# A new written order of steps for a Nystrom attention and feed-forward kernel, with a changed planner's clock

## The chip, the cores and the metric

The kernel runs on one core of one Trainium2 chip. The metric is the device time of one execution in microseconds (us). The median of several runs is compared before and after the change; lower is better.

The engines are called as in the profile: PE is TensorE (PEld its weight loads), DVE is VectorE, ACT is ScalarE, POOL is GpSimd, SP is SyncE, whose queue issues most of the DMAs.

## The reference

There are 8 batches of 576 rows, with 8 heads of 64 columns. For each head, 32 landmarks are the means of 18 rows each, and three softmax matrices and an iterated inverse give the attention:

```
q_lm, k_lm = means of 18 rows of q, of k
A, Bm, C = sm(q, k_lm), sm(q_lm, k_lm), sm(q_lm, k)
Z = Bm^T / (norm1(Bm) * norminf(Bm))
for _ in range(6): Z = 2 Z - Z Bm Z
x = A Z C v                      # heads side by side: 576 x 512 for each batch
xn = (x - mean) / sqrt(var + 1e-6) * g
out = x + relu(xn @ w1) @ w2     # w1 512 x 2048, w2 2048 x 512
```

Everything comes in and goes out as fp32; the kernel multiplies in fp16.

## The kernel before

**Stages.** The batches are taken in sets: batch 0 in code of its own, then (1), (2), (3, 4), (5, 6) and (7). For a set, q, k and v are loaded (tiles stg, a ring of six buffers that W1, W2 and the mixed W2 share), cast to fp16 by POOL or sometimes ACT (tiles nat and natv), turned by DVE (xT) and summed to landmarks (DVE's part, POOL's asum, or products on PE, bank<-nat,pairs). Then come the score products (psec, psea), their exponentials (ec, ea), the Gram product and six iterations for Z (tile st: a small product on PE, then one DVE operation, six times in a row), the product with v (pscv), and zt and zcbd, from which the rows of the attention's output are made (xblk). DVE measures each block of 128 rows (bn_stats into six, bn_aggr into stats).

**The feed-forward part.** The first layer does not use the rows: it multiplies zt with W1 (two products of heads give m), then m with ea, 16 chunks of hidden units for each batch (psh), which are passed through Relu into hT. The second layer multiplies hT with W2, 16 matmuls for a block of 128 rows, and adds the result, scaled, to xblk, which is then stored. For batches 4 to 7 four of the blocks are replaced by seven products of mixed quarters (bank<-w2mix and so on); DVE makes the mixed hT, POOL the mixed W2.

**The centerings.** For batches 0 and 1 the mean over W1's rows (less) is subtracted when m is copied out. From batch 2 on W1 itself is centered: `center_w1` (line 1484) adds less to two of the four parts of a quarter of W1, 1024 elements in each of 128 partitions, in one DVE operation. There are eight of these (DVE w<-w,less). Batch 2's first layer may not begin before all eight are written (line 1864, `first_layers`).

**What sets the order.** Each engine runs its instructions in the order in which the program lists them, and semaphores hold an instruction until its inputs are there. The order is written by hand: `ORDER` (line 1828) is a list of symbols with counts, run by `run` (line 1922). A symbol is a step:

- 0 to 4 are streams: 0 the attentions (from set (1) on), 1 the totals on PE, 2 the first layers, 3 the rows of batch 0, 4 the second layers. A step passes one `yield` of its stream. A step of 4 is mostly one matmul of 512 columns, or one of 256 in the seven products; a step of 2 mostly four matmuls of 288.
- J is a turn or a sum on DVE, M measures a block, C is a centering, X mixes a part of hT, W a part of W2, K casts and L loads one tile of 576 KB.

So "42 2 L" means two steps of the second layer, one of the first and a load. A step that can't be written yet (its input isn't made, or its buffers are all pinned) goes to a list `late` and is tried again after each following step. A buffer stays pinned from its load until its cast is written. `settle` writes the stores of finished blocks as soon as the clock says that they are done; they go to SP's queue, as the loads do.

**The planner's clock.** While the program is written, `Clock` (line 85) notes every instruction and keeps an estimate of when each engine is free and each tile is written. This is a calculation in Python; no instruction comes from it. But choices hang on it: whether ACT or DVE copies a result (`sooner`, line 635, and `chunk`, line 1540), whether an attention step is an iteration or something beside it, when a store goes out, whether a filler matmul is put in (`warm`), and whether ACT takes a cast. It knows that some DVE operations of 1024 elements and POOL's operations hold each other up (`locks`, and `took` for n of 1024).

Ahead of `run` stands a fixed part: batch 0's attention, the loads of W1 and W2 and their casts. It is not in the list.

Of the kernel before, what the change touches and what calls it, by code (L numbers as in the profile page):

```python
# [20 lines left out]
def kernel(  # L21
# [20 lines left out]
    MCH = HID // P  # L42
# [30 lines left out]
    def keys_of(ap):  # L73
        n = name_of(ap)
        if n not in parted:
            return [n]
        at = [ap.offset % list(ap.ap)[0][0]]
        for step, k in list(ap.ap)[1:]:
            if step >= parted[n]:
                at = [o + step * i for o in at for i in range(k)]  # L80
        if n in mixed_:
            return [f"{n}:{o // parted[n]}:{int(o % parted[n] >= 256)}" for o in at]
        return [f"{n}:{o // parted[n]}" for o in at]

    class Clock:
# [5 lines left out]
        def __init__(self):  # L91
            self.free = dict.fromkeys(("PE", "DVE", "Activation", "Pool", "SP"), 0.0)
            self.wrote, self.used, self.begun = {}, {}, {}
            self.small, self.lanes, self.wire = False, {}, 0.0
            self.cells, self.count, self.mark, self.fetched, self.ahead = [], 0, 95, 0.0, 0.0
            self.loads, self.pool = [], []
            self.locks = []
            self.free['PE'], self.issued = 1500.0, 0

        def share(self, span=3400.0):  # L100
# [31 lines left out]
        def took(self, i, e, n, m):  # L132
            op = type(i).__name__
            if e == "Activation":
                return 300 if n < 8 else 190 + (1.07 if name_of(i.outs[0].bass_ap).startswith("ec_") else 0.79) * n
            if e == "Pool":
                if n == 1024 and name_of(i.outs[0].bass_ap) in mixed_:
                    return 2080
                if "Ptr" in op:
                    return 100 + 1.29 * n  # L140
                return 100 + 0.92 * n if "Copy" in op else 280 + 1.76 * n
            if "Copy" in op and n in (256, 384, 512, 640) and name_of(i.outs[0].bass_ap).startswith("xT"):
                return 90 + 0.58 * n
            if n == 1152 and "Copy" in op:
                return 760
            if n == 576 and "Copy" in op and name_of(i.outs[0].bass_ap).startswith("nat_"):
                return 400
            if "Stats" in op:
                return 690 if m > 100 else 180
            if n >= 512 and (n == 576 or op == 'InstTensorCopy'):  # L150
                return 100 + 1.13 * n
            if n == 1024:
                last = max([b for a, b in self.pool if a <= self.ready < b] + [0.0])
                next_ = self.locks and self.ready - self.locks[-1][1] < 150
                queued = (690 if self.free["Pool"] <= self.ready else
                          1600 if next_ and self.free["Pool"] > self.ready + 1000 else 1000)
                return max(queued, last - self.ready + 560)
            if n == 256 and "Ptr" in op and name_of(i.outs[0].bass_ap).startswith("xblk"):
                return 480
            if "Transpose" in op:  # L160
                return 110 + 1.15 * n
            return 140 + 1.15 * max(n, m if "Reduce" in op else 0)

        def note(self, i):
            e = str(i.engine).rsplit(".", 1)[-1]
# [3 lines left out]
            count = []  # L169
            for dims in size:  # L170
                n = 1
# [63 lines left out]
                    done = self.lanes[lane[0]] + 160  # L235
            else:
                start = max(self.free[e], ready)
                if e == "Pool":
                    for a, z in self.locks:
                        if a <= start < z:  # L240
                            start = z
                self.ready = start
                done = start + self.took(i, e, count[0], max(count[1:] + [0]))
                self.free[e] = done - self.OVERLAP[e]
                if e == "Pool":
                    self.pool = self.pool[-8:] + [(start, done)]
                    self.free["DVE"] += sum(done - a for a, _ in self.locks[-2:] if start < a < done)
# [1444 lines left out]
    def mix_ahead():  # L1692
# [6 lines left out]
        if i == 0:  # L1699
            n = hTs[b].name  # L1700
            mixed_.update((name_of(s1), name_of(s2), n))
            for seen in (clock.wrote, clock.used):
                seen.update({f"{n}:{m}:{h}": seen[f"{n}:{m}"] for m in range(MCH) for h in range(2)
                             if f"{n}:{m}" in seen})
            mix(s1, h21, h22, ALU.add, k)
        elif i == 1:
# [111 lines left out]
    def scaled_by_pe():  # L1818
# [7 lines left out]
    begun_first = [0]  # L1826

    ORDER = (
# [18 lines left out]
    ).split()  # L1847
    JOB, MEASURE, CENTER, MIX, MIX_W2, CAST, LOAD = range(5, 12)

# [173 lines left out]
```

## Time and profile before

| | us |
|---|---|
| three runs: median (lowest to highest) | 262.17 (261.54 to 262.8) |
| profiled execution | 262.2 |
| its span, first to last instruction | 260.5 |
| busy: PE, DVE, ACT, POOL | 251.2, 206.9, 172.3, 139.7 |

The mean granted TensorE clock is 1.00. In a line of the timeline the columns are start and length in us, engine, line, operation and tiles, with a count; the square bracket holds the idle time of the engine just before and what ended it. A line of the chain has start, length, and engine with the tile written. All helpers record at lines 316 (DVE, ACT, POOL) and 322 (PE), so the tiles' names tell instructions apart. "w<-w,less" is a centering, "m<-less,zsum,bank" a copy with the mean subtracted, "bank<-w,hT" the second layer, "psh<-ea,m" the first.

### The profile page before, as it was taken

The page shows a single profiled execution, that of the slowest core. Times are in us where ns is not written, and L with a number is a line of the kernel's source. Part 1 is how long each engine was busy: PE and PEld are TensorE (multiplying, and loading weights), DVE is VectorE, ACT ScalarE, POOL GpSimd, SP SyncE. Part 2 cuts the span into 40 slices and gives each one's busy share as a digit, 9 for nine tenths or more (in the row PEclk, how much of TensorE's full clock was granted, in tenths as well). Part 3 has the DMA queues.
Part 4 walks back from the last instruction along what each step waited for, and adds up shares of the span by engine and source line. Part 5 has one row for each costly group of instructions (what it writes and reads, how often), then busy time and mean ns, then how long its engine had stood idle before and what let it go on. Part 6 is the DMA issues. An engine that isn't in the chain of part 4 may idle for free.

```text
span 260.5 us, 8627 instructions
## 1 busy us (share of the span) xinstructions
PE 251.2 (96%) x3551; PEld 167.8 (64%) x3551; DVE 206.9 (79%) x470; ACT 172.3 (66%) x330; POOL 139.7 (54%) x165
## 2 busy tenths in 40 slices
PE   6899999999999999999999999999999999999994
PEld 6645754556455574546655466688878876788883
DVE  2667966999989978999997794987495997398862
ACT  2798975559767987289987668636788835786000
POOL 5188779999990989679999996300000006000000
PEclk9999999999999999999999999999999999999999
DMA  6999999997966899658961101200240025100605
GB/s 243 374 397 371 402 402 383 359 331 228 347 195 204 279 374 284 184 168 242 286 154 43 37 10 40 63 22 0 57 108 3 4 55 119 33 3 3 160 21 184
DMA packets 23119, 46.70 MB, mean 179 GB/s; under 512 B 2980, under 2 KB 3240, under 8 KB 23080
## 3 DMA queue, kind: packets, MB, share of 16 engines
q1 hardware_dynamic: 22600, 45.50, 54.3%
q10 hardware_dynamic: 480, 0.66, 0.8%
q8 instruction: 28, 0.46, 0.7%
q14 instruction: 11, 0.09, 0.1%
HBM read 36.70 MB, written 9.44 MB: 177 GB/s over the span
## 4 chain that ended last, share of the span: by engine, by line
PE 70%; DVE 13%; DMA 8%; POOL 4%; issue 1%; ACT 1%; SPq 1%; POOLq 0%
PE bank L322 45%; PE psh L322 18%; DMA stg<-in_q_dram 5%; DMA wstg<-in_moe_w_ch_dram 3%; POOL w L316 3%; PE pscv L322 2%; DVE m L316 2%; DVE xblk L316 2%; DVE w L316 2%; PE psd L322 2%; DVE part L316 1%; DVE six L316 1%; POOL ea L316 1%; DMA out_dram<-xblk 1%; DVE st L316 1%
## 5 line engine op out<-in xcount | busy, mean ns | idle before, releaser
L322 PE MATMUL bank<-w,hT 128*128 128x512 f16 (+3 forms) x528 | 110.1, 335 | 0.2 <-POOL w L316 0.2
L316 ACT ACTIVATE hT<-psh 128x576 f16<-128x576 f32 x124 | 78.1, 652 | 19.1 <-PE psh L322 16.9
L322 PE MATMUL psh<-ea,m 128*128 128x288 f16 x512 | 80.0, 286 | 0.3 <-DVE m L316 0.2
L322 PEld LDWEIGHTS <-hT 128*128 128x128 f16 x656 | 60.2, 98 | 29.9 <-issue 5.0
L322 PEld LDWEIGHTS <-m 128*128 128x128 f16 x512 | 49.4, 98 | 18.8 <-issue 1.3
L316 POOL TENSOR_TENSOR ea<-ea,lns 128x576 f16<-128x576 f16 x16 | 20.9, 1314 | 56.5 <-ACT lns L316 56.4
L316 DVE SCALAR_TENSOR_TENSOR xblk<-bank,rstd,xblk 128x256 f32<-128x256 f32 (+2 forms) x77 | 38.9, 539 | 12.2 <-PE bank L322 11.9
L316 POOL CAST nat<-stg 128x1152 f16<-128x1152 f32 x26 | 30.3, 1182 | 9.3 <-DVE xT L316 7.0
L316 DVE BATCH_NORM_STATS2 six<-xblk 128x6 f32<-128x512 f32 x36 | 24.3, 674 | 0.1
L316 POOL CAST natv<-stg 128x1152 f16<-128x1152 f32 (+1 forms) x17 | 19.3, 1162 | 8.5 <-DMA stg<-in_v_dram 8.4
L316 DVE STREAM_TRANSPOSE xT<-nat 128x576 uint32<-128x576 uint32 x28 | 21.3, 760 | 0.0
L316 DVE SCALAR_TENSOR_TENSOR st<-st,bank 128x128 f16<-128x128 f16 (+3 forms) x36 | 13.2, 366 | 7.1 <-PE bank L322 6.9
L316 ACT ACTIVATE lns<-psd 128x576 f32<-128x576 f32 x16 | 10.3, 645 | 12.3 <-PE psd L322 12.1
L322 PE MATMUL bank<-w2mix,hT 128*128 128x256 f16 x128 | 18.0, 273 | 0.0
L322 PE MATMUL bank<-w2mix 128*128 128x256 f16 x128 | 17.3, 273 | 0.0
L316 DVE TENSOR_REDUCE part<-xT 128x32 f16<-128x576 f16 x20 | 14.4, 741 | 0.0
L322 PEld LDWEIGHTS <-w2mix 128*128 128x128 f16 x128 | 12.3, 98 | 1.9
L316 ACT ACTIVATE ea<-psea 128x576 f16<-128x576 f32 x14 | 8.3, 648 | 7.9 <-PE psea L322 7.9
L322 PEld LDWEIGHTS <-st 32*32 32x32 f16 (+1 forms) x380 | 6.8, 90 | 9.9 <-DVE st L316 5.1
L316 ACT ACTIVATE ec<-psec 128x256 f16<-128x256 f32 (+1 forms) x42 | 12.0, 427 | 1.7 <-PE psec L322 1.6
L316 ACT COPY xblk<-bank 128x512 f32<-128x512 f32 (+1 forms) x16 | 9.3, 592 | 5.6 <-PE bank L322 5.6
L316 POOL TENSOR_TENSOR asum<-nat 128x512 f32<-128x512 f16 x10 | 12.5, 1249 | 0.8
(132 smaller groups left out, 372.4 us busy)
## 6 DMA issues: line engine op xcount, KB each, us to landing
stg<-in_q_dram SPq DMA_DIRECT2D x16, 576.0 KB, 6.4
stg<-in_k_dram SPq DMA_DIRECT2D x15, 576.0 KB, 5.6
out_dram<-xblk SPq DMA_DIRECT2D x66, 128.0 KB, 2.4
wstg<-in_moe_w_ch_dram SPq DMA_DIRECT2D x16, 512.0 KB, 7.5
stg<-in_v_dram SPq DMA_DIRECT2D x5, 576.0 KB, 7.4
stg<-in_v_dram SPq DMA_DIRECT2D x40, 72.0 KB, 3.1
stg<-in_v_dram SPq DMA_DIRECT2D x6, 288.0 KB, 6.2
stg<-in_v_dram SPq DMA_DIRECT2D x12, 144.0 KB, 3.1
```

The lines of the kernel that those rows point to most:

```text
L316: return lambda *args, **kw: keep(getattr(self.engine, op)(*args, **kw))
L322: keep(nc.tensor.matmul(o, l, r, start=start, stop=stop, tile_position=(rb, cb), skip_group_check=(skip or cb != 0)))
```

## The change

The list is replaced by another of the same steps: 1337 in both, with the same number of each symbol. Beyond order, these things differ: the old list begins with the first layer of batch 0 and spreads its loads, while the new one begins with ten loads; the eight centerings, the measurements, casts and attention steps have other places among the steps of the first and second layers.

The places of the eight centerings, by the number of second-layer steps (symbol 4) written before each: 18, 21, 50, 58, 63, 90, 93, 94 in the old list and 16, 27, 49, 57, 87, 91, 92, 93 in the new. The step that holds batch 2's Gram product (the 22nd of stream 0) comes after 66 in the old and 70 in the new.

In the clock, DVE's operations on 1024 elements now look back at all of POOL's operations that run at the time; POOL's operations already noted are pushed back when a DVE operation holds them (`hold_pool`); a POOL operation that starts within such a DVE operation ends later instead of starting later; all DVE tensor_tensor operations of 1024 elements count, not only the centerings; and ACT's scaling of W1 is taken at 750 ns. A mixed hT is tracked in three parts of 256 columns (the third shorter) instead of two.

The diff, cut to its core:

```diff
@@ keys_of
-            return [f"{n}:{o // parted[n]}:{int(o % parted[n] >= 256)}" for o in at]
+            return [f"{n}:{o // parted[n]}:{int(o % parted[n] // 256)}" for o in at]
@@ Clock.took
+                if n == 512 and name_of(i.outs[0].bass_ap).startswith("w1_16"):
+                    return 750
...
-                last = max([b for a, b in self.pool if a <= self.ready < b] + [0.0])
-                next_ = self.locks and self.ready - self.locks[-1][1] < 150
-                queued = (690 if self.free["Pool"] <= self.ready else
-                          1600 if next_ and self.free["Pool"] > self.ready + 1000 else 1000)
-                return max(queued, last - self.ready + 560)
+                return max([690] + [p[1] - self.ready + 545 for p in self.pool
+                                    if p[0] <= self.ready < p[1]])
...
+        def hold_pool(self, start, done):
+            free = 0.0
+            for p in self.pool:
+                if p[0] <= start:
+                    continue
+                was = p[1]
+                if p[0] < free:
+                    p[0] = free
+                    p[1] = p[0] + p[2]
+                if p[0] < done:
+                    p[1] = max(p[1], done + p[2] - 140)
+                free = p[1] - self.OVERLAP["Pool"]
...
+            self.free["Pool"] = max(self.free["Pool"], free)
@@ Clock.note
-                    for a, z in self.locks:
-                        if a <= start < z:
-                            start = z
+                    done = max([done] + [z + took - 140 for a, z, _ in self.locks if a <= start < z])
+                    for lock in self.locks:
+                        if start < lock[0] < done and done + 545 > lock[1]:
+                            lock[1] = done + 545
+                            self.free["DVE"] = max(self.free["DVE"], lock[1] + self.worked - lock[2] - 80)
...
-                if e == 'DVE' and count[0] == 1024 and writes[0] in parted_w1:
-                    self.locks = self.locks[-4:] + [(start, done)]
+                if e == 'DVE' and count[0] == 1024 and "TensorTensor" in type(i).__name__:
+                    self.locks = self.locks[-6:] + [[start, done, self.worked]]
+                    self.hold_pool(start, done)
@@ ORDER (the first lines of each)
-        "2 3 4 211 M 32 25 3 J 0 J3 22 J3 2 1 2 3 22 L 2 M 2 1 2 1 2 J 2 1 4 2 3 L 4 0 42 2 0 "
-        "4 23 0 4 L 0 4 02 4 L M 4 04 L 4 0 K 0 L 42 2 M 0 43 L 42 K 0 C 22 J 0 4 K J K 42 C "
-        "4 2 J 42 2 L 42 0 2 J 43 2 4 M 43 K 45 J 4 L J2 K J 0 2 J 4 J L2 0 4 2 L 4 L 2 M 4 2 "
-        "M L 4 2 4 K M 2 L 4 2 4 2 4 2 0 M 2 42 2 K C 48 0 2 C 45 C 4 L 4 K 4 0 4 K 4 K2 0 47 "
-        "1 04 L 43 02 4 J 43 0 43 L2 K 4 0 4 J 4 1 0 42 K 2 C L 42 0 L 4 C 4 C 44 K 0 L 2 4 J "
...
+        "L5 3 L5 0 210 3 M 3 25 M 4 22 J 2 J 23 J 2 J 2 M J 2 J 2 1 32 M J 0 2 1 2 1 4 2 1 2 "
+        "4 3 J 42 0 2 4 22 0 4 03 42 0 2 03 4 02 2 4 0 K 44 K 4 C 42 0 22 42 0 K J2 4 K 4 2 4 "
+        "2 44 C 0 J 4 0 4 K 2 J 2 J2 44 M2 42 J 0 43 J K J 4 J 2 M2 K 4 M 4 2 42 22 42 2 42 "
+        "22 42 2 C 2 0 4 L 43 L 44 L C 4 2 4 L 2 K L 0 42 K 43 L2 44 K3 4 L 4 02 44 02 L 4 0 "
+        "43 0 4 0 J 1 0 4 0 2 43 K2 4 0 2 4 J K 42 1 0 C 4 L 43 0 C M 4 K C 4 C L 43 K 4 0 L "
...
```

Both lists end with 181 steps of the second layer in a row.

More of the change, by code (lines that the diff above doesn't have):

```diff
@@ L96, in __init__ @@
             self.loads, self.pool = [], []
-            self.locks = []
+            self.locks, self.worked = [], 0.0
             self.free['PE'], self.issued = 1500.0, 0
@@ L162, in took @@
             return 140 + 1.15 * max(n, m if "Reduce" in op else 0)
+        def hold_pool(self, start, done):
[10 more added lines that the diff above has]
+                free = p[1] - self.OVERLAP["Pool"]
+                if p[1] > was:
+                    for at, names in ((self.used, p[3]), (self.wrote, p[4])):
+                        for n in names:
+                            if at.get(n) == (was, "Pool"):
+                                at[n] = p[1], "Pool"
+            self.free["Pool"] = max(self.free["Pool"], free)
         def note(self, i):
@@ L237, in note @@
                 start = max(self.free[e], ready)
+                self.ready = start
+                took = self.took(i, e, count[0], max(count[1:] + [0]))
+                done = start + took
                 if e == "Pool":
-                    for a, z in self.locks:
-                        if a <= start < z:
-                            start = z
-                self.ready = start
-                done = start + self.took(i, e, count[0], max(count[1:] + [0]))
-                self.free[e] = done - self.OVERLAP[e]
-                if e == "Pool":
-                    self.pool = self.pool[-8:] + [(start, done)]
-                    self.free["DVE"] += sum(done - a for a, _ in self.locks[-2:] if start < a < done)
-                if e == 'DVE' and count[0] == 1024 and writes[0] in parted_w1:
-                    self.locks = self.locks[-4:] + [(start, done)]
+                    done = max([done] + [z + took - 140 for a, z, _ in self.locks if a <= start < z])
[3 more added lines that the diff above has]
+                            self.free["DVE"] = max(self.free["DVE"], lock[1] + self.worked - lock[2] - 80)
+                    self.pool = self.pool[-24:] + [[start, done, took, reads, writes]]
+                self.free[e] = done - self.OVERLAP[e]
+                if e == "DVE":
+                    self.worked += done - start - self.OVERLAP[e]
+                if e == 'DVE' and count[0] == 1024 and "TensorTensor" in type(i).__name__:
+                    self.locks = self.locks[-6:] + [[start, done, self.worked]]
+                    self.hold_pool(start, done)
             for n in reads:
@@ L1702, in mix_ahead @@
             for seen in (clock.wrote, clock.used):
-                seen.update({f"{n}:{m}:{h}": seen[f"{n}:{m}"] for m in range(MCH) for h in range(2)
+                seen.update({f"{n}:{m}:{h}": seen[f"{n}:{m}"] for m in range(MCH) for h in range(3)
                              if f"{n}:{m}" in seen})
```

26 rows, old and new, of the table ORDER are left out of this document.

## The prediction

> **What bounds the kernel now.** I read the engine table of the page and its chain first.
>
> ```profile
> span 260.5 us, 8627 instructions
> ...
> PE 251.2 (96%) x3551; PEld 167.8 (64%) x3551; DVE 206.9 (79%) x470; ACT 172.3 (66%) x330; POOL 139.7 (54%) x165
> ...
> PE 70%; DVE 13%; DMA 8%; POOL 4%; issue 1%; ACT 1%; SPq 1%; POOLq 0%
> ```
>
> TensorE (PE) is busy for all but 9.3 us of the span and holds 70% of the chain that ended last. A busy PE need not be a streaming one, so the next view is the timeline of a stretch in the middle.
>
> ```profile
> 179.72 0.65 PE L322 MATMUL psh<-ea,m 128*128 128x288 f16 x4
> 180.21 0.38 PE L322 MATMUL bank<-w2mix,hT 128*128 128x256 f16 x2
> 180.43 0.65 PE L322 MATMUL psh<-ea,m 128*128 128x288 f16 x4
> ```
>
> Four matmuls of 288 columns are followed after 0.49 us, and two of 256 columns after 0.22 us. That is 0.122 and 0.110 us a piece, in proportion to the columns (0.42 and 0.43 ns each), so nothing but columns is being paid for. The record of a group runs 0.16 us past the start of the next (0.65 against 0.49). So whatever the page calls PE idle hides up to 0.16 us more at each place. Next, the busy time by stage (columns: stretch; its length; then each engine's busy time and count).
>
> ```profile
> 18.20:50.00 31.80, 30.85 (x420) 17.50 (x421) 24.84 (x64) 23.83 (x49) 27.62 (x29) 1.00 1.03 390
> 50.00:66.00 16.00, 16.00 (x156) 9.73 (x160) 15.76 (x31) 12.06 (x23) 15.29 (x18) 1.00 0.91 275
> 66.00:74.00 8.00, 7.01 (x129) 3.60 (x108) 7.70 (x20) 4.75 (x13) 7.45 (x9) 1.00 0.92 331
> 74.00:250.00 176.00, 175.85 (x2475) 120.59 (x2474) 145.63 (x318) 120.79 (x234) 79.83 (x80) 1.00 0.40 113
> ```
>
> The third number is PE. What precedes 18.2 us is written ahead of the list of steps, and behind 250 us runs the end of the second layer, 181 steps in a row in both lists. Between lies what an order can touch: PE idles 0.95 us in 18.2 to 50, nothing in 50 to 66, 0.99 us in 66 to 74, and 0.15 us in the 176 us after. That is 2.1 us, and with 0.16 us hidden at some seven places about 3.2 us. VectorE (DVE) is full from 50 to 74, but PE waits for it only in the one stretch of 8 us.
>
> **The change part by part.** The list keeps its 1337 steps, and as many of each kind (830 of the second layer, 165 of the first, 117 of the attentions, 36 loads, 36 casts, 8 centerings). The edits to the clock, to its locks and to its three keys for the mixed hT emit nothing; they only steer the planner's choices (which engine copies, when a store goes out, a filler matmul). I cost them at nothing. A copy that goes to DVE instead of ScalarE (ACT) lies on engines that do not hold PE in 74 to 250 us; where DVE is full, it counts among the waits of the last part below.
>
> *Ten loads at the head of the list.* Six can be taken at once, since the ring stage has six buffers; the others come out with the casts that free one. But already before, the first load waits for its buffer, not for its place:
>
> ```profile
> 39.20 1.04 POOL L316 CAST w<-wstg 128x1024 f16<-128x1024 f32 x1 [0.59 <-DMA wstg<-in_moe_w_ch_dram]
> 40.27 1.60 SPq L331 DMA_DIRECT2D stg<-in_k_dram  x2
> ```
>
> The cast ends at 40.24 and the load goes out at 40.27. So the first six gain nothing. The four behind them are written some steps earlier on SP's queue, ahead of the stores of batch 0. Those stores then wait until GpSimd (POOL) has done its cast; what waits for them is a block buffer that batch 2's rows want only after 80 us. Bounds: 0 and one cast, 1.1 us, both beside PE work; I take 0.
>
> *The rows of batch 0* come after ten steps of the first layer instead of twelve.
>
> ```profile
> 18.23 0.53 PE L322 MATMUL bank<-w,zt 64*32 64x512 f16 x8 [0.27 <-DVE zt L316]
> ...
> 19.15 1.32 PE L322 MATMUL psh<-ea,m 128*128 128x288 f16 x8 [0.18 <-DVE m L316]
> ...
> 23.64 0.38 PE L322 MATMUL bank<-zcbd,ea 128*128 128x256 f16 x2 [0.21 <-DVE m L316]
> ...
> 45.28 0.39 PE L322 MATMUL bank<-w,zt 64*32 64x512 f16 x1 [0.29 <-DVE zt L316]
> ```
>
> These four are the 0.95 us of the stage. The first two stand where both lists still run the same first steps. The third waits until DVE's copies of m free a bank; two row products (0.22 us each) now come before it, so the next matmul of the mean meets the same bank earlier. It saves 0.37 (idle and hidden part) at best and loses as much as those 0.43 us at worst; I take 0. The fourth stays: in both lists the product of batch 1 is asked for before its zt exists, and is let out right behind it.
>
> *The centerings before batch 2's Gram product.* This is the place where the order changes what PE waits for. The chain of waits from 66 us on:
>
> ```profile
> 69.23 2.13 DVE w L316 x2
> 71.36 0.15 DVE csum L316
> ...
> 71.73 0.43 DVE st L316
> ...
> 72.21 0.31 PE bank L322 x2
> ```
>
> and what PE did there:
>
> ```profile
> 66.25 1.90 PE L322 MATMUL bank<-w,hT 128*128 128x512 f16 x8
> ...
> 68.48 0.29 PE L322 MATMUL bank<-st 128*128 128x128 f16 x2 [0.29 <-DVE st L316]
> ...
> 70.84 0.67 PE L322 MATMUL bank<-nat,pairs 128*128 128x128 f16 x9
> 72.21 0.31 PE L322 MATMUL bank<-st 128*128 128x160 f16 x2 [0.70 <-DVE st L316]
> ```
>
> The two DVE w are centerings 4 and 5 of W1; csum, and with it the first iteration of batch 2, stands behind them. In the old list centerings 4 and 5 come after 58 and 63 second-layer steps, the Gram step after 66. In the new list centering 4 comes after 57, the Gram step after 70, and centering 5 only after 87. So one centering leaves DVE's queue ahead of csum. It is the dear one:
>
> ```profile
> L316 DVE TENSOR_TENSOR w<-w,less x8: 644/810/1625, 48.6 to 80.6; 128x1024 f16<-128x1024 f16 x8
> 69.18 1.63 POOL L316 CAST nat<-stg 128x1152 f16<-128x1152 f32 x1
> ...
> 74.17 1.14 POOL L316 CAST nat<-stg 128x1152 f16<-128x1152 f32 x1
> ```
>
> At 69 us a centering took up to 1.63 us (the shortest 0.64) beside a cast that took 1.63 us (alone 1.14). DVE had st ready at 71.73 + 0.43 = 72.16, and now has it 1.63 earlier, near 70.5. PE: a second-layer step is (1.90 - 0.16)/8 = 0.22 us. The Gram step comes four such steps later, 0.87 us, which covers its wait of 0.45 (0.29 idle, 0.16 hidden). Before the first iteration PE has one second-layer step less (74 for 75) and the product of totals (0.67 - 0.16 = 0.5 us) not yet. Its wait there was 0.86 (0.70 and 0.16). Without both waits PE got there at 72.21 - 0.86 - 0.45 = 70.9; with 0.22 + 0.5 less to do it gets there at 70.2 and waits 0.3 us. The stage gives back 0.45 + 0.86 - 0.3 = 1.0 us. Bounds: 0.45 lost, if a later step meets what is left of DVE's backlog, and 1.3 gained.
>
> The Trainium skill, SBUF — State Buffer, section Who interferes with whom, says that a DVE instruction with two SBUF inputs and a GpSimd instruction that reads SBUF exclude each other, and that whichever starts later blocks until the first has finished. The rows of 69 us agree: both are stretched. By that rule a moved centering saves or costs only what it finds on POOL in its new place, and that speaks against the change in the next paragraph.
>
> *The centerings bunch up.* Centerings 5 to 8 now stand after 87, 91, 92 and 93 second-layer steps, and five casts after 83 to 96; before, three centerings stood at 90 to 94 and two casts. What the three cost then:
>
> ```profile
> 78.71 0.68 DVE L316 TENSOR_TENSOR w<-w,less 128x1024 f16<-128x1024 f16 x1
> ...
> 79.97 1.28 DVE L316 TENSOR_TENSOR w<-w,less 128x1024 f16<-128x1024 f16 x2
> 84.82 1.14 POOL L316 CAST nat<-stg 128x1152 f16<-128x1152 f32 x1 [7.03 <-DVE xT L316]
> ```
>
> They ran while POOL was idle (77.8 to 84.8), 0.66 us each. Four at 0.66 add 0.66 us to DVE there, which the second layer's matmuls of batch 1 hide; four beside casts, at 1.06 as at 52.2 us, would add 4 x 1.06 - 1.96 = 2.3.
>
> ```profile
> 52.21 1.06 DVE L316 TENSOR_TENSOR w<-w,less 128x1024 f16<-128x1024 f16 x1
> 80.00:90.00 10.00, 10.00 (x80) 6.12 (x79) 9.82 (x20) 8.80 (x17) 5.18 (x5) 1.00 0.69 225
> ```
>
> PE had no idle time there, but DVE had only 0.18 us, so this cover is thin. I take 0, bounds 0 and 2.3.
>
> *The rest.* Behind 100 second-layer steps the attention steps are grouped much as before: 0.15 us of idle in 176 us leaves nothing to gain, and each new meeting of PE with an unfinished input is a loss of 0.1 to 0.7 us like those above. I take 0, bounds 0.15 gained and 1.5 lost (about what three or four such waits cost).
>
> Sum: -1.0 + 0 + 0 + 0 + 0 = -1.0 us. The profiled execution took 262.2 us with a span of 260.5, so 1.7 lies around it; the median of the runs is 262.17, and both give 261.2.
>
> **The rivals.**
>
> *More is found (259.9).* The Gram pair goes entirely (1.3 us), the waits at 23.6 (0.37) and 45.3 (0.29 + 0.16) shrink, and so do the last 0.15. That is 2.3 us. For it: the waits are there. Against it: the last two places are written alike in both lists.
>
> *The wait only moves (262.2).* DVE is full from 50 to 74 (7.70 of 8, 15.76 of 16); what one step no longer waits for, the next iteration does. Then the 1.0 us comes back within batch 2's iterations and the time stays. For it: the iterations now stand singly and hang on the same DVE. Against it: a centering really leaves this stretch.
>
> *Slower (264.0): centerings beside casts.* Four centerings and five casts in one place, each stretched as at 69 us: DVE falls 2.3 us behind and up to 4 x 1.63 - 1.96 = 4.6. It is full there, so batch 2's first copies of m and the transposes for batches 3 and 4 come late, and PE, which takes its steps in the written order, stands still. With half of the worst case beyond the cover, 2.8 us, less the 1.0 us if that is gained still: 262.2 + 2.8 - 1.0 = 264.0. It decides once DVE is later than the second-layer steps written in between, some five or 1.1 us. For it: DVE's 9.82 of 10. Against it: ACT can take the copies of m. The rule on the shared port in the Trainium skill, SBUF — State Buffer, section Who interferes with whom, makes the stretching certain wherever a centering meets a cast, and so speaks for this case.
>
> That the change does nothing is no case: the order of instructions on every queue changes.
>
> **How the numbers follow.** Forecast 0.40, more 0.17, moved 0.16, slower 0.27. The likeliest gives 261.2. A measurement of this kernel can tell about 0.5%, 1.3 us (260.9 to 263.5). The forecast's own spread, 260.2 to 262.6, lies a third below 260.9: faster 0.17 + 0.13 = 0.30. Slower 0.27. Within: 0.16 + 0.27 = 0.43. The range reaches from 259.3 (a little more than 2.3 us gained) to 265.2 (the slower case with 4.0 instead of 2.8).
>
> **What would show it.** Right: no DVE w between batch 2's Gram product and its csum, and PE idle in 66 to 74 us down from 0.99 to about 0.3; the loads' issue still at the end of a w2 cast; four DVE w close together near 78 to 83 us, each under 0.8 us; PE in 74 to 250 still within 0.5 us of full. Wrong: PE idle over 1 us in 78 to 95 behind DVE m or DVE xT, with DVE w over 1 us beside a POOL cast (the slower case); new waits of PE in the stages of batches 3 to 7, which I have put at nothing; or a PE busy as before with a longer span, which would mean more changes between small and whole tiles than I counted.

## The result and the profile after

| | before | after |
|---|---|---|
| median us (lowest to highest), 16 runs each | 262.14 (261.52 to 263.23) | 261.12 (260.6 to 261.91) |
| profiled execution, us | 262.2 | 260.8 |
| its span, us | 260.5 | 259.0 |

The ratio of after to before is 0.9965, with a 95% interval of 0.9952 to 0.9977: 0.9 us faster, between 0.6 and 1.3. The interval excludes no change, and the gain is within the 0.5% that the prediction called the same.

In the changed kernel the helpers record at lines 339 (DVE, ACT, POOL) and 345 (PE). The page after, from its engine table and the engines of its chain:

```profile
PE 250.5 (97%) x3551; PEld 168.3 (65%) x3551; DVE 204.3 (79%) x465; ACT 173.5 (67%) x334; POOL 140.8 (54%) x166
...
PE 90%; DVE 4%; DMA 2%; POOL 1%; issue 1%; ACT 1%; SPq 0%; DVEq 0%; ACTq 0%; POOLq 0%
```

PE runs the same 3551 matmuls, and its share of the chain went from 70% to 90%: between 46 and 72 us the chain ran mostly over DVE before, and now runs over PE. The busy time by stage (stretch; length; PE, PE's weight loads, DVE, ACT, POOL; granted clock; DMA):

```profile
18.20:50.00 31.80, 30.51 (x419) 17.51 (x420) 24.45 (x64) 24.12 (x50) 28.13 (x29) 1.00 1.03 388
...
66.00:74.00 8.00, 7.98 (x160) 4.48 (x149) 7.23 (x20) 5.46 (x13) 7.45 (x10) 1.00 0.94 327
74.00:250.00 176.00, 176.00 (x2483) 121.59 (x2482) 144.78 (x313) 121.13 (x237) 80.51 (x80) 1.00 0.39 112
```

PE's idle time fell from 0.99 to 0.02 us in 66 to 74, from 0.15 to nothing behind it, and rose from 0.95 to 1.29 us in 18.2 to 50. The gain is in the stretch where the prediction looked for it, and a part of it is paid back earlier. DVE and then PE around batch 2's Gram product and its first iteration:

```profile
69.56 0.18 DVE L339 TENSOR_REDUCE csum<-bank 128x2 f32<-128x64 f32 x1
...
69.97 0.42 DVE L339 TENSOR_TENSOR st<-bank,cinv 128x256 f16<-128x256 f32 x1
```

```profile
68.99 0.28 PE L345 MATMUL bank<-st 128*128 128x128 f16 x2
...
69.61 0.82 PE L345 MATMUL bank<-w,hT 128*128 128x512 f16 x3
70.45 0.31 PE L345 MATMUL bank<-st 128*128 128x160 f16 x2
70.70 0.72 PE L345 MATMUL pscv<-natv,ecT 64*64 64x130 f16 x36
```

No centering stands between the Gram product (68.99) and csum (69.56). The st of the first iteration is written at 69.97 + 0.42 = 70.39, and that iteration starts at 70.45. The three matmuls ahead of it end their streaming at 69.61 + 0.82 - 0.16 = 70.27, so PE waits 0.18 us there, nearly all of it inside what the page counts as busy. Before, the same iteration started at 72.21. It is 1.76 us earlier, of which 0.72 is work that moved behind it (one second-layer step and the product of totals). That leaves 1.04 us.

The centerings after, as one group (shortest, median, longest in ns), then DVE and POOL where the last four stand:

```profile
L339 DVE TENSOR_TENSOR w<-w,less x8: 675/800/984, 48.2 to 80.0; 128x1024 f16<-128x1024 f16 x8
```

```profile
76.60 0.91 DVE L339 TENSOR_TENSOR w<-w,less 128x1024 f16<-128x1024 f16 x1
...
78.75 1.88 DVE L339 TENSOR_TENSOR w<-w,less 128x1024 f16<-128x1024 f16 x3
```

```profile
76.90 1.60 POOL L339 CAST nat<-stg 128x1152 f16<-128x1152 f32 x1
83.10 1.15 POOL L339 CAST nat<-stg 128x1152 f16<-128x1152 f32 x1 [4.59 <-DMA stg<-in_v_dram]
```

The longest centering is 0.98 us where it was 1.63. Of the last four only the first meets POOL. It begins within POOL's product for ea (74.31 to 76.96) and takes 0.91 us; the cast at 76.90 begins within the centering and takes 1.60 us, where a cast alone takes 1.14 or 1.15. Then POOL waits 4.59 us for a load, and the other three run alone, 0.63 us apart (a record is 0.68 us long, and the records overlap).

PE in 18.2 to 50, its two waits that are new or longer:

```profile
23.68 1.04 PE L345 MATMUL bank<-w,lesser 128*128 128x512 f16 x4 [0.42 <-DVE m L339]
...
44.41 0.22 PE L345 MATMUL pszc<-cv,st 32*32 32x64 f16 x8 [0.36 <-ACT lns L339]
```

The rows of batch 0 come two steps sooner, and the matmul of the mean behind them waits 0.42 us for DVE's copies of m; before, one of the row products waited 0.21 there. At 44.41 batch 1's product pszc waits 0.36 us for a logarithm of ACT, lns; before, the wait near that place was 0.29 us for zt at 45.28. SP's queue:

```profile
39.80 1.60 SPq L354 DMA_DIRECT2D stg<-in_k_dram  x2
...
57.24 2.79 SPq L1467 DMA_DIRECT2D out_dram<-xblk  x4
```

The first loads go out at 39.80 (before 40.27), still when a cast of W2 has freed their buffer, and batch 0's stores stand behind loads that now come first, at 57.24. No engine is listed as waiting for them.

### The profile page after: what moved, and what is told of

Its sections match the earlier page's. It is cut to its first block, busy times and chain, and to the rows that moved or that the text cites. A ratio compares the mean times of both kernels' runs of the same rounds, so it can differ in the third digit from the quotient of the medians.

```text
span 259.0 us, 8621 instructions
## 1 busy us (share of the span) xinstructions
PE 250.5 (97%) x3551; PEld 168.3 (65%) x3551; DVE 204.3 (79%) x465; ACT 173.5 (67%) x334; POOL 140.8 (54%) x166
## 4 chain that ended last, share of the span: by engine, by line
PE 90%; DVE 4%; DMA 2%; POOL 1%; issue 1%; ACT 1%; SPq 0%; DVEq 0%; ACTq 0%; POOLq 0%
PE bank L345 58%; PE psh L345 23%; DMA stg<-in_q_dram 2%; PE pscv L345 2%; PE psd L345 2%; DVE m L339 1%; PE psec L345 1%; PE psea L345 1%; PE psr L345 1%; DVE xT L339 1%; POOL w L339 1%; ACT lns L339 1%; DVE six L339 0%; PE pszt L345 0%; SPq L354 0%
## 5 line engine op out<-in xcount | busy, mean ns | idle before, releaser
L339 ACT ACTIVATE hT<-psh 128x576 f16<-128x576 f32 x122 | 76.1, 651 | 21.7 <-PE psh L345 20.5
L339 POOL CAST nat<-stg 128x1152 f16<-128x1152 f32 x27 | 31.5, 1179 | 9.2 <-DMA stg<-in_v_dram 4.6
L345 PE MATMUL bank<-w2mix,hT 128*128 128x256 f16 x128 | 17.2, 273 | 0.0
L339 ACT COPY xblk<-bank 128x512 f32<-128x512 f32 (+1 forms) x21 | 12.2, 597 | 5.6 <-PE bank L345 5.5
L339 ACT CAST m<-bank 128x512 f16<-128x512 f32 x20 | 11.3, 589 | 4.0 <-PE bank L345 3.7
L339 POOL TENSOR_TENSOR asum<-asum 128x256 f32<-128x256 f32 (+1 forms) x20 | 12.2, 608 | 1.6
```

The costliest lines, as they stand in the source:

```text
L339: return lambda *args, **kw: keep(getattr(self.engine, op)(*args, **kw))
L345: keep(nc.tensor.matmul(o, l, r, start=start, stop=stop, tile_position=(rb, cb), skip_group_check=(skip or cb != 0)))
```

## The experiments

The theory on trial: the time comes from DVE's queue in front of batch 2's iterations, by one centering less and a Gram product later, and it stays gained because the later centerings have cover. The rivals: the wait only moves; the clustered centerings cost as much as they save; or the gain comes from some other part of the new list, or from the clock's choices, which the prediction had put at nothing. Each kernel ran 12 or 13 times and is compared with the kernel before on the same chip, which ran 35 times beside each of the three sets (medians 262.68, 262.37 and 262.32 us). Kernels whose names begin with b start from the kernel before, those with a from the kernel after. In most of them one centering is taken from its place and written at another, and everything else is to stay as it was. For that the list has two more symbols: G stands at the old place and only tells the planner's clock that the centering is written there, so that all its choices stay; D writes the instruction without telling the clock. In the traces of experiments 1 to 3 DVE, ACT and POOL run the instructions of the kernel they start from in the same order, but for that one centering.

**1. The centering away (b_c5_away).** The old list; the fifth centering leaves the Gram product's neighbourhood and comes after 88 second-layer steps. The new list has it after 87, but behind the step of batch 2's last iteration (`0 C`); here it stands ahead of that step (`D 1 0`).

```diff
- "... C 45 C 4 L 4 K ..."        "... J 4 1 0 42 K 2 C ..."
+ "... C 45 G 4 L 4 K ..."        "... J 4 D 1 0 42 K 2 C ..."
```

> The old order with one instruction moved: the fifth centering leaves its place ahead of batch 2's csum on VectorE's queue and comes after 88 second-layer steps, as in the new order; every other instruction on every engine keeps its place. Theory (the centering ahead of csum is what TensorE waits for): the idle time before the first iteration of batch 2 (0.70 us in the old order) goes, the one before the Gram product (0.29) stays, TensorE idles 0.3 us in 66 to 74 us, and the time falls by 0.7 to 0.9 us. Rival (the wait only moves to the next iterations): idle time of 0.7 us or more turns up in 72 to 80 us and the time stays within 0.2 us. Rival (centerings close together are dear): the time rises, with TensorE idle in 78 to 95 us.

262.07 us, ratio 0.9979 (0.9953 to 1.0005), which is not to be told from the kernel before. PE is busy for all 8.00 us of 66 to 74 (the wait at the Gram product, which was to stay, is absent in this execution), but a few microseconds on there is this, on DVE and on PE:

```profile
76.67 0.98 DVE L316 TENSOR_TENSOR w<-w,less 128x1024 f16<-128x1024 f16 x1
77.57 0.21 DVE L316 SCALAR_TENSOR_TENSOR st<-st,bank 128x64 f16<-128x64 f16 x1
```

```profile
77.83 0.24 PE L322 MATMUL pszt<-st,cv 32*32 32x32 f16 x16 [0.63 <-DVE st L316]
```

The centering has landed just ahead of the last of the six steps of Z, whose result pszt needs: the wait of 0.70 us at the first iteration has become one of 0.63 us at the end of the chain. Here the rival "the wait only moves" is seen at work, by the choice of one place.

**2. One step later still (b_c5_later).** The same, with the centering behind the last iteration, as in the new list.

```diff
- "... J 4 1 0 42 K 2 C ..."
+ "... J 4 1 0 D 42 K 2 C ..."
```

> The old order with the fifth centering behind batch 2's last iteration (in b_c5_away it stood just ahead of that, and a wait of 0.63 us came up at 77.8 us, where TensorE waited for the last st). Nothing else moves. Theory: the idle time before the first iteration (0.70 us) goes and none comes up at 77 us; the time falls by 0.7 to 1.0 us against the kernel before. Rival (VectorE is full here, so the wait goes on moving): idle time of 0.5 us or more between 77 and 95 us, and a fall of under 0.4 us.

261.74 us, ratio 0.9971 (0.9955 to 0.9987): 0.8 us faster by the ratio, between 0.3 and 1.2. The stretch from 66 us:

```profile
66.00:74.00 8.00, 7.74 (x135) 4.01 (x116) 6.72 (x20) 5.62 (x15) 7.45 (x10) 1.00 0.92 329
74.00:82.00 8.00, 7.96 (x90) 4.17 (x89) 7.54 (x15) 5.83 (x12) 3.46 (x3) 1.00 0.68 181
```

The wait at the first iteration is gone and does not come back; the Gram product's stays (0.26 idle). So one DVE instruction out of the queue in front of csum is worth most of the change's gain, if it does not fall in front of another step of the chain.

**3. The centering back (a_c5_back, a_c5_back_again).** The new list, with the fifth centering put back ahead of csum.

```diff
- "... 42 1 0 C 4 L 43 0 C M ..."      "... K L 0 42 K 43 L2 ..."
+ "... 42 1 0 G 4 L 43 0 C M ..."      "... K L 0 42 K D 43 L2 ..."
```

> The new order with one instruction moved back: the fifth centering stands again ahead of batch 2's csum (written after 61 second-layer steps instead of 87); nothing else moves. Theory: VectorE has st ready 0.7 to 1.0 us later than now (70.4), TensorE, which arrives at 70.4, waits that long, and the time rises by 0.6 to 1.0 us. Rival (the gain comes from the four more second-layer steps ahead of the Gram product and from the finer split of the iterations): the rise is under 0.3 us.

> The kernel of a_c5_back once more, beside the changed kernel on the same chip: its first profile is of an execution of 265.1 us, far above its median of 262.3. Theory (the centering ahead of csum makes TensorE wait): a profile with 0.6 to 1.0 us of TensorE idle before the first iteration of batch 2, and a time 0.6 to 1.0 us above the changed kernel. Rival (the gain is from the other parts of the new order): under 0.3 us above it.

262.27 us in the first set (0.9969, 0.9948 to 0.999) and 262.71 in the second (1.0007, 0.999 to 1.0024). The second set holds the changed kernel itself as well (after_again).

> The changed kernel once more, as the measure for the others of this call. Expected: 1.0 us under the kernel before (ratio 0.995 to 0.998), TensorE idle in 66 to 74 us under 0.2 us.

It took 261.08 us, ratio 0.9956 (0.9936 to 0.9976). So putting the centering back costs 1.6 us there by the medians and 1.3 by the ratios: the whole gain. The first set, which did not hold the changed kernel, is less clear: its ratio leaves a_c5_back 0.8 us below the kernel before (0.3 to 1.4). DVE and POOL, then PE, of a_c5_back_again:

```profile
64.44 2.24 POOL L339 CAST nat<-stg 128x1152 f16<-128x1152 f32 x2
...
65.75 1.48 DVE L339 TENSOR_TENSOR w<-w,less 128x1024 f16<-128x1024 f16 x1
...
70.43 1.14 POOL L339 CAST nat<-stg 128x1152 f16<-128x1152 f32 x1
...
70.94 1.18 DVE L339 TENSOR_TENSOR w<-w,less 128x1024 f16<-128x1024 f16 x1
```

```profile
70.25 0.29 PE L345 MATMUL bank<-st 128*128 128x128 f16 x2 [0.49 <-DVE st L339]
...
72.97 0.31 PE L345 MATMUL bank<-st 128*128 128x160 f16 x2 [1.27 <-DVE st L339]
```

The returned centering (70.94) takes 1.18 us beside a cast and PE waits 1.27 us for what stands behind it. The 0.49 at the Gram product has another cause: in this execution the third centering, which was not touched, started at 65.75 within POOL's casts and took 1.48 us (in the kernel after 0.69, from 65.14). In the profile of a_c5_back it took 1.64 us, and PE waited 1.14 us at the Gram product and 0.92 at the first iteration. So 0.5 us or more of what these executions lost is the meeting of an untouched pair. Taken off the 1.3 to 1.6 us, that leaves 0.8 to 1.1 us for the instruction itself, near the 1.0 us of the prediction; this is a subtraction, and no run shows it alone.

**4. The Gram product's place (b_c5_gram).** Kernel 2 with the Gram step after 70 second-layer steps as well; the iterations of batch 2 then follow in pairs.

```diff
- "C 45 C 4 L 4 K 4 0 4 K 4 K2 0 47 "
+ "C 45 G 4 L 4 K 42 K 4 K2 42 02 45 "
```

> b_c5_later with the Gram step after 70 second-layer steps instead of 66 as well, as in the new order; by that TensorE takes the product with v ahead of the first iteration, and POOL makes a cast that ACT made. Theory: the idle time before the Gram product (0.29 us) goes too, TensorE idles under 0.1 us in 66 to 74 us, and the time falls by 1.1 to 1.4 us against the kernel before, as far as the whole change or further. Rival (other parts of the new order give the gain): it falls no further than b_c5_later, and stays 0.5 us or more above the changed kernel.

263.0 us, ratio 1.0016 (0.9998 to 1.0033): 1.3 us slower than the kernel of experiment 2 by the medians. Both old waits are gone, and two others have come:

```profile
73.18 0.42 PE L322 MATMUL psd<-ea,bones 128*128 128x288 f16 x2 [0.44 <-DVE cv L316]
...
74.97 0.31 PE L322 MATMUL bank<-st 128*128 128x160 f16 x2 [0.58 <-DVE st L316]
```

I had expected a gain beyond kernel 2. A step that does not wait itself runs into the next one's input earlier: to move the Gram product later without moving the second-layer steps that stood between the iterations opens the chain behind it. That is read from this trace alone: the product with v also comes ahead of the first iteration here (71.53 and 72.18), and the run does not part the two causes. Experiments 5 and 6 show the second of them.

**5. The whole stage in the old list (b_stage).** Centering, Gram product and the single iterations written as in the new list, in the old list and with the old clock.

```diff
- "C 45 C 4 L 4 K 4 0 4 K 4 K2 0 47 1 04 L 43 02 4 J 43 0 43 L2 K 4 0 4 J 4 1 0 42 K 2 C"
+ "C 45 G 4 L 4 K 42 K 4 K2 42 02 44 02 L 4 0 43 0 4 0 J 1 0 4 0 43 L2 K 4 0 4 J 42 1 0 D 43 K 2 C"
```

> The old order with batch 2's stage alone written as in the new one: the fifth centering behind the last iteration, the Gram step after 70 second-layer steps, and the iterations with second-layer steps between them (b_c5_gram wrote them in pairs, and TensorE then waited 0.44 and 0.58 us between them). The product with v comes ahead of the first iteration. Theory (the gain of the change is that stage, all three parts together): TensorE idles under 0.2 us in 66 to 74 us and under 0.2 in 74 to 82, and the time falls by 1.0 to 1.4 us against the kernel before. Rival (the rest of the new order gives part of it): a fall of 0.7 us or less, with the idle time gone all the same.

261.8 us, ratio 0.9986 (0.9968 to 1.0003): about 0.4 us, less than half of what was expected and not to be told from nothing. DVE and PE:

```profile
73.22 0.77 DVE L316 STREAM_TRANSPOSE xT<-nat 128x576 uint32<-128x576 uint32 x1
```

```profile
74.43 0.31 PE L322 MATMUL bank<-st 128*128 128x160 f16 x2 [0.54 <-DVE st L316]
```

A transpose, xT, stands in front of an iteration's DVE step, and PE has only one second-layer step to do meanwhile. In the kernel after the same transpose meets an iteration that has four such steps behind it:

```profile
73.57 0.77 DVE L339 STREAM_TRANSPOSE xT<-nat 128x576 uint32<-128x576 uint32 x1
...
74.06 1.03 PE L345 MATMUL bank<-w,hT 128*128 128x512 f16 x4
```

What differs is the step in front: here the clock chose to write the product with v (pscv) before the first iteration, and so every iteration is one place later among the second-layer steps.

**6. The new list with the old clock (a_clock).** It tests that directly.

```diff
  the kernel before, with ORDER replaced by the new list
```

> The new list with the old clock. The prediction took the edits to the clock at nothing. The programs differ in one place: with the old clock the planner puts the product with v and one normalization ahead of batch 2's first iteration, where the changed kernel has the iteration first. TensorE then has 0.7 us more work ahead of it and does not wait there (0.14 us idle in the changed kernel); what follows comes later. Theory: within 0.3 us of the changed kernel, 0.7 to 1.2 us under the kernel before. Rival (the changed clock is needed for the gain): waits of 0.5 us or more after the product with v, and no gain over before.

261.85 us by the median, 0.5 below the kernel before; the ratio is 0.9999 (0.9982 to 1.0016), no gain. DVE's step in front of PE's longest wait is again the transpose. PE, and the table of stages:

```profile
70.95 0.72 PE L322 MATMUL pscv<-natv,ecT 64*64 64x130 f16 x36
...
72.07 0.30 PE L322 MATMUL bank<-st 128*128 128x160 f16 x2
...
75.26 0.31 PE L322 MATMUL bank<-st 128*128 128x160 f16 x2 [0.53 <-DVE st L316]
```

```profile
66.00:74.00 8.00, 7.87 (x157) 4.30 (x155) 6.83 (x19) 6.52 (x17) 7.45 (x10) 1.00 0.92 343
74.00:82.00 8.00, 7.39 (x87) 3.71 (x85) 7.04 (x14) 3.79 (x10) 4.44 (x4) 1.00 0.65 192
```

The same picture as in b_stage: pscv first (70.95), the first iteration only at 72.07, and the wait behind xT. PE idles 0.13 + 0.61 us in the two stretches where the kernel after idles 0.02 (0.14 in its second execution, after_again). Against the kernel after, DVE has one step of Z in another place, ACT one copy, POOL nothing, and PE the iterations against the product with v and what hangs on it. So the new list without the changed clock is worth 0.5 us at best, and the rest of the gain is the clock's choice of what to write first.

**7. The rows of batch 0 (a_rows12).** The new list with these rows after twelve steps of the first layer, as before.

```diff
- "L5 3 L5 0 210 3 M 3 25 M"
+ "L5 3 L5 0 212 3 M 3 23 M"
```

> The new order with the two row products of batch 0 after twelve steps of the first layer again instead of ten; only TensorE's order changes, by four matmuls. The prediction took 0 for this part, between 0.37 saved and 0.43 lost by the new place. By the trace of the new order, where the wait for the bank grew from 0.21 to 0.42 us idle: the old place gives 0.2 us back, and the time falls by 0.2 us. Rival (the later casts and loads set when the next products can start): no change, since a later wait in 18 to 50 us takes the gain up.

261.28 us, ratio 0.994 (0.992 to 0.996). PE at that place:

```profile
23.82 0.38 PE L345 MATMUL bank<-zcbd,ea 128*128 128x256 f16 x2 [0.20 <-DVE m L339]
```

The wait is back at 0.20 from 0.42. The ratio is lower than that of the kernel after in its own comparison (0.9965) and in the other set (0.9956), but the intervals overlap, and the medians point the other way: 0.2 us is not to be told from nothing here.

**8. The loads first (b_loads_first).** The old list, with ten loads at its head and its first ten L left out.

> The old order with its first ten loads at the head of the list, as in the new order; only SP's queue changes, where three loads pass in front of stores of batch 0. Theory (the loads wait for their buffers, not for their place): the first six go out at the times of before, the stores of batch 0 move from 51 us to about 57, nothing on TensorE moves, and the time stays within 0.2 us. Rival (earlier loads feed the casts of batches 3 and 4 earlier, and that is part of the gain): the time falls by 0.3 us or more. Rival (the late stores hold block buffers): it rises.

262.38 us, ratio 0.9989 (0.9967 to 1.0011). The first loads go out at 39.82 and batch 0's stores at 57.45, as in the kernel after, and PE is busy 7.01 us in 66 to 74, as before. No worth of the loads is to be seen, either way.

**9. More work for DVE (a_dve_more).** The kernel after, with two maxima of a tile with itself behind the eighth centering. They leave the values as they are.

```diff
- "C M 4 K C 4 C L 43 K"
+ "C M 4 K C 4 C G L 43 K"
+ G: for c in (0, 2): dve.tensor_tensor(out=o, in0=o, in1=o, op=max),  o = w1_16[:, c:c+2, 3*512:4*512]
```

> The changed kernel with two operations more on VectorE behind the eighth centering: each takes the greater of a part of W1 and itself, in place, 1024 elements in 128 partitions, so that the result stays the same. That adds 1.3 us to VectorE near 80 us. It measures the cover that the prediction's slower case counted on at 1.1 us. Theory (ScalarE takes the copies and second-layer steps stand between): TensorE idles under 0.3 us in 78 to 95 us, and the time rises by under 0.3 us. Rival (VectorE is full there and TensorE waits for it): 0.7 to 1.3 us more.

261.32 us, ratio 0.9951 (0.9933 to 0.997). DVE, and the table of stages:

```profile
81.40 1.28 DVE L339 TENSOR_TENSOR w<-w 128x1024 f16<-128x1024 f16 x2
```

```profile
74.00:82.00 8.00, 8.00 (x97) 4.51 (x95) 7.43 (x14) 5.84 (x13) 5.28 (x5) 1.00 0.64 178
82.00:250.00 168.00, 168.00 (x2391) 117.01 (x2389) 139.25 (x303) 116.11 (x226) 76.00 (x76) 1.00 0.39 110
```

DVE has 1.28 us more in front of everything that follows, and PE still does not idle. The cover at the clustered centerings is at least 1.3 us, though DVE is busy for nearly all of that stretch (9.89 of 10 us from 80 to 90).

**10. An attempt at a better version (a_best).** The kernel of experiment 7, and two second-layer steps moved ahead of batch 1's zt, where PE waits near 44 us.

```diff
- "4 02 2 4 0 K 44 K 4 C"
+ "4 02 2 43 0 K 42 K 4 C"
```

> The changed kernel with two edits to its list, which only change TensorE's order: the row products of batch 0 after twelve steps again (a_rows12), and two second-layer steps moved ahead of batch 1's zt step, where TensorE waited 0.36 us at 44.4 us for a buffer that ScalarE still read. Theory: 0.2 us from the first and 0.4 from the second, 0.4 to 0.6 us under the changed kernel and 1.4 to 1.8 under the kernel before. Rival (a wait that is filled comes back later): within 0.2 us of the changed kernel.

262.78 us, ratio 1.0018 (1.0005 to 1.0031): instead of a gain, about 1.7 us slower than the kernel after by the medians (1.4 to 1.6 by the ratios). DVE of this kernel, DVE of the kernel after, and PE of this kernel:

```profile
49.09 1.68 DVE L339 TENSOR_TENSOR w<-w,less 128x1024 f16<-128x1024 f16 x1
...
53.47 1.07 DVE L339 TENSOR_TENSOR w<-w,less 128x1024 f16<-128x1024 f16 x1
...
55.82 0.70 DVE L339 SCALAR_TENSOR_TENSOR m<-less,zsum,bank 128x512 f16<-128x512 f16 x1
...
69.76 1.28 DVE L339 TENSOR_TENSOR st<-bmT,mask 128x256 f16<-128x256 f16 x1
```

```profile
48.20 0.97 DVE L339 TENSOR_TENSOR w<-w,less 128x1024 f16<-128x1024 f16 x1
...
51.88 0.92 DVE L339 TENSOR_TENSOR w<-w,less 128x1024 f16<-128x1024 f16 x1
...
54.27 0.75 DVE L339 SCALAR_TENSOR_TENSOR m<-less,zsum,bank 128x512 f16<-128x512 f16 x1
...
68.32 0.49 DVE L339 TENSOR_TENSOR st<-bmT,mask 128x256 f16<-128x256 f16 x1
```

```profile
45.74 0.39 PE L345 MATMUL bank<-w,zt 64*32 64x512 f16 x1 [0.42 <-DVE zt L339]
...
56.58 0.81 PE L345 MATMUL bank<-w,hT 128*128 128x512 f16 x3 [0.23 <-DVE m L339]
...
71.10 0.28 PE L345 MATMUL bank<-st 128*128 128x128 f16 x2 [0.61 <-DVE st L339]
```

The two steps did not fill the wait: the one of 0.36 us for lns went, and just behind it PE waits 0.42 us for zt (45.74). DVE begins this stretch 0.9 us later (0.44 of it is from before the list begins: the product at 18.20 starts at 18.64 in this execution), and its first two centerings meet POOL differently: 2.75 us together instead of 1.89. So the copy of m at 54.27 starts at 55.82, 1.55 us later, and the second layer waits for it at 56.58. DVE is full from there on and 1.44 us late at the mask of batch 2's Gram product, which in its new place takes 1.28 us instead of 0.49 (POOL casts from 69.62 on); PE waits 0.61 us for it at 71.10. That the meeting with the cast stretched it is read from the overlap, not shown by a run of its own. No version that is measurably faster than the kernel after was found.

## Why the prediction was right

*The centerings before batch 2's Gram product (-1.0).* Right in mechanism and size. Both waits went, the centering left the queue, PE idles 0.02 us, and the first iteration starts 1.04 us earlier, net of the moved work (predicted 1.0). In this the 0.28 us of longer waits before 50 us are paid already, so the stage alone gave a little more. The remaining wait was put at 0.3 us and is 0.18. Doing the one move alone in the old list brought most of the gain (experiment 2). Undoing it brought PE's wait back and took the gain away in the second set; the first set leaves open how much of it (experiment 3).

*The edits to the clock cost nothing.* This step was wrong. I argued that a choice of the clock could only move a copy between engines that do not hold PE. But the clock also chooses whether an attention step is the iteration or the product with v, and in batch 2 this decides which iteration stands behind the transpose with one second-layer step for cover. Where it chose the other way, PE idled 0.74 us in 66 to 82 (a_clock) and 0.32 + 0.43 = 0.75 (b_stage), where the kernel after idles 0.02: three quarters of the predicted gain. The sum came out because the forecast had taken the better order (iteration first) for granted, as it was before. That part of the hit is luck: nothing in the prediction said why the order would stay.

*Ten loads (0).* Right: issue still at the end of a cast, the stores later, nobody waiting; alone they change nothing that the time or PE's waits show.

*The rows of batch 0 (0, between -0.37 and +0.43).* On the losing side: 0.2 us by the trace, too small for the timing.

*The centerings bunch up (0, up to 2.3).* Right in the sum. Three of the four met no cast, because POOL was waiting for a load, which the prediction had not foreseen; the first took 0.91 us, more than the 0.8 it named. And 1.3 us of further DVE work there cost nothing: the cover is wider than DVE's 9.82 of 10 us of busy time suggested, and the 1.1 us at which the slower rival was to decide is too low. The delay of 2.3 us and more that it foresaw did not arise, and no run tested it.

*The rest (0, between -0.15 and +1.5).* The listed 0.15 us of idle time behind 74 went; no new wait came up there. The span shrank by 1.5 us, 1.04 of it up to the first iteration. The other 0.46 would be the 0.15 and two hidden parts of 0.16 us; that is arithmetic and was not tested. The fourth wait before 50 us, which the prediction let stay, is now the one for lns at 44.41 (0.36 for 0.29).

*The rivals.* "More is found" did not occur: the Gram pair went but the two early waits grew. "The wait only moves" is false for this change and true for close neighbours of it (experiments 1, 4 and 5). "Centerings beside casts" names a real price, but at other places: 1.48 us from 65.75 on, within POOL's casts (experiment 3), against 0.68 in the three that ran alone. The Trainium skill, SBUF — State Buffer, section Who interferes with whom, has a DVE operation with two SBUF inputs and a GpSimd operation that reads SBUF exclude each other, and these rows agree. What I had not drawn from it is that the centerings of 48 to 66 us, which the change hardly moves, are as exposed as the four at the end.

What stays open: how the 0.9 to 1.2 us divide among the centering, the Gram product's place and the clock, since they depend on each other (the centering alone 0.6 to 0.8 by median and ratio, the stage without the clock 0.4 to 0.5, the list without the clock 0 to 0.5), and whether the rows' 0.2 us are real in the time.

## What to carry to other kernels

Where one engine is full and the bound engine waits for it at a chain of small dependent steps, look at which instruction stands in front of the chain's step in the other engine's queue, and move that one behind the chain's last step, not between two of its steps. Before a wait is filled with work, ask what the next dependent step then has for cover: in experiments 1, 4 and 10 a wait came up elsewhere, and in the last two the kernel was slower than the one it started from. And a planner's internal estimate that emits nothing can still decide which of two steps comes first, so compare the order of instructions that comes out, not only the edits.

## What the runs showed that was not expected

The same centering, with the same neighbours on its own queue, took 0.69 us in the kernel after, 0.80 in a second execution of it and 1.48 in a_c5_back_again, whose change is written behind it. What differs is where it starts against the end of POOL's casts: 0.16, 0.26 and 0.93 us ahead of it. Each time it ended 0.53 to 0.55 us after the casts did (65.83 after 65.30, 66.36 after 65.82, 67.23 after 66.68). DVE, busy for 15.16 of 16 us from 50 to 66 in that last execution, passed the difference on: PE waited 0.49 us at the Gram product. Why this centering met POOL so in both executions with the fifth one put back (1.64 us in the other) is not shown.

The profiled execution of a_c5_back took 265.12 us, 2.85 above the median of its runs, so it is no measure of that kernel; its stages show a granted clock (the third number from the end) below 1:

```profile
66.00:74.00 8.00, 5.93 (x118) 2.61 (x120) 7.79 (x16) 4.89 (x13) 7.45 (x10) 0.96 0.96 353
74.00:82.00 8.00, 8.00 (x106) 4.67 (x97) 5.38 (x13) 3.25 (x7) 4.38 (x5) 0.83 0.64 173
```

```profile
75.39 1.49 PE L345 MATMUL bank<-w,hT 128*128 128x512 f16 x3
```

After 8.00 - 5.93 = 2.07 us of idle time within 66 to 74, three second-layer matmuls took (1.49 - 0.16)/3 = 0.44 us each, twice the usual 0.22. By an estimate from the mean of 0.83 over 8 us this is worth some 1.4 us. The same kernel in the second set idled 1.75 us in that stretch at a clock of 1.00. Whether the idle time brought the clock down, and what decides it, is not shown.
